# The last down stage: two PSUM tiles with two halves each, or eight banks with a quarter each

## The chip, the core and the metric

One core of a Trainium2 chip runs the whole kernel. The metric is the device time in microseconds (us) of one execution; the time of a kernel is the median over its runs.

## The reference

A retention layer feeds a mixture of four two-layer networks. Reduced to what matters here:

```python
# x: (4608, 512), the retention output of 8 batches x 576 tokens, heads side by side
p = domain_probs / (domain_probs.sum(-1, keepdims=True) + 1e-09)   # (4608, 4)
out = zeros((4608, 512))
for e in range(4):
    h = maximum(x @ w1[e], 0)          # w1[e]: (512, 1024)
    out += p[:, e:e+1] * (h @ w2[e])   # w2[e]: (1024, 512)
```

Inputs and output are float32. The kernel multiplies in bfloat16 and accumulates in float32.

## The kernel before

The 4608 tokens are nine tiles of 512 (`nt`), and for each tile there are four experts (`e`), so there are 36 stages. A stage has an up product (tokens times w1, then relu, into `hT`, hidden features on the partitions) and a down product (`hT` times w2). The down product of a stage is issued between the pieces of the up product of the next stage (`up_fast` and its `fill`), so that TensorE always has one to run while the other is being emptied. The order is written out by hand: every engine runs its instructions in the order in which the program issues them, and waits are semaphores between engines. The last stage (tile 8, expert 3) has no up product behind it, so its down product stands alone at the end of the program, in the loop at L1120 to L1136.

From the second tile on most products use a scheme with seven block products instead of eight. For the down product a set of 256 rows by 512 columns is cut into quarters 11, 12, 21 and 22 (rows: tokens in the first or the second half of the tile; columns: the first or the second 256 of 512). `Down` (L624) does this for one set of 128-token blocks; `s` is 0 or 1, and set `s` holds the token blocks `s` and `s + 2` of the tile. The parts of the scheme:

- Sums on VectorE beforehand: `hidden_sum` (L616, L618, L620, L622) makes sums of blocks of `hT`; `down_sums` has made sums of blocks of w2 (`dsum`).
- `product(i)`, i from 1 to 7: four matmuls of 128x128 by 128x256 each (L644). Products 1 and 2 add up quarter 11, 3 and 5 belong to quarter 12, and 4, 6 and 7 to quarters 21 and 22.
- `copy`: ScalarE copies product 1 into the place of the second row's sum ("P1", L650), so that product 6 adds onto it; it keeps product 5 in SBUF ("m5", L657) and the sum of products 1 and 6 ("U", L654).
- `add`: VectorE adds U to quarter 12 and m5 to quarter 22 (L661).
- `out`: a finished row of 512 columns is multiplied by the token's weight and added to `acc` (L673), since for the last tile (`on_chip`) the sum over the experts stays in SBUF; after the last expert it is sent to `out` (L680).

PSUM has eight banks, named P, Q, R, o0, o1, a0, a1 and a2. In `Down` the tile V holds quarters 11 and 12 in one bank, and W holds 21 and 22 in another. For the last stage set 0 has V in o0 and W in o1, which the stage before used for its own down product, and set 1 has them in P and Q, which the up product used. The banks a0, a1 and a2 were used by the attention and are idle by then. The loop at L1121 issues product 1 of both sets, then product 5 of both sets with the P1 and m5 copies behind each, then 6, 2, 7, 3 and 4. After product 3 the first row is finished in two halves, each with an accumulation on VectorE and a transfer of 128 KB issued by SP; after product 4 the second row likewise. All eight transfers go through SP's queue, which waits for VectorE ahead of each. The end of the program (L1162 in the profile) waits for all transfers on SP and joins the engines.

Of the kernel before, what the change touches and what calls it, by code (L numbers as in the profile page):

```python
# [9 lines left out]
FP32 = mybir.dt.float32  # L10
BF16 = mybir.dt.bfloat16
Copy = mybir.ActivationFunctionType.Copy
Relu = mybir.ActivationFunctionType.Relu
Exp = mybir.ActivationFunctionType.Exp
MULT = mybir.AluOpType.mult
ADD = mybir.AluOpType.add
# [7 lines left out]
def kernel(  # L24
# [10 lines left out]
    nc = tc.nc  # L35
    B, H, S, D = q.shape
    N, E = moe_domain_probs.shape
    _, Dm, F = moe_w1.shape
    assert (B, H, S, D) == (8, 8, 576, 64) and (N, E, Dm, F) == (4608, 4, 512, 1024)
    scale = 1.0 / math.sqrt(D)  # L40
    C = 128
    NCH = S // C
    R = S - NCH * C
# [3 lines left out]
    NFC = F // 128  # L47
    NT = 512
    n_nt = N // NT
    NSUB = NT // 128  # L50
# [7 lines left out]
    raw = ctx.enter_context(tc.tile_pool(name="raw", bufs=RAW))  # L58
# [5 lines left out]
    tpool = ctx.enter_context(tc.tile_pool(name="tpool", bufs=1))  # L64
# [12 lines left out]
    def one_bank(tag, shape, dtype, name):  # L77
        return psum.tile(shape, dtype, tag=tag, name=name)
# [63 lines left out]
    w1_sb, w2_sb = [], []  # L142
# [71 lines left out]
    probs = const.tile([128, E, NTT], FP32)  # L214
# [36 lines left out]
    class Att:  # L251


        def __init__(self, b):
            self.b, self.t = b, state[b]
            self.m, self.qkT, self.sT, self.s = {}, {}, {}, {}
# [243 lines left out]
    def on_chip(nt):  # L500
        return nt in (0, n_nt - 1)

    def out_pair(nt, e, pair, j):

        if e == 0 or not on_chip(nt):
            acc[nt, j] = apool.tile([128, 2, Dm], FP32, tag="acc", name="acc")
        return acc[nt, j]

    def send(nt, e, pair, j):
        x = slice(nt * NSUB + pair[0], nt * NSUB + pair[1] + 1, pair[1] - pair[0])  # L510
        if e == 0:
            i = nc.sync.dma_start(out=out_rows[:, x, :], in_=acc[nt, j])
        else:
            i = nc.gpsimd.dma_start(out=out_rows[:, x, :], in_=acc[nt, j], accum_op=ADD)  # L514
            for p, d in sent[nt, e - 1]:
                if set(p) & set(pair):
                    after(i, d)
        sent.setdefault((nt, e), []).append((pair, i))

    acc, hTs, tsum, ssum, dsum, hsum = {}, {}, {}, {}, {}, {}  # L520
# [57 lines left out]
    HF, HT, HD = F // 2, NT // 2, Dm // 2  # L578
# [28 lines left out]
    def hidden_sum(nt, e, i, g=None):  # L607

        lo, hi = (slice(2 * g, 2 * g + 2), slice(4 + 2 * g, 6 + 2 * g)) if g is not None else (slice(0, 4), slice(4, 8))
        hT = hTs[nt, e]  # L610
        a11, a12, a21, a22 = (hT[:, k, t] for t in (slice(0, HT), slice(HT, NT)) for k in (lo, hi))
        h = hsum.setdefault((nt, e), {})
        if i != 3 and i not in h:
            h[i] = hpool.tile([128, NFC // 2, HT], BF16, tag=f"hs{i}", name="hsum", bufs=1)
        if i == 1:
            nc.vector.tensor_tensor(h[1][:, lo], a21, a22, op=ADD)  # L616
        elif i == 2:
            nc.vector.tensor_tensor(h[2][:, lo], h[1][:, lo], a11, op=SUB)  # L618
        elif i == 3:
            nc.vector.tensor_tensor(a21, a11, a21, op=SUB)  # L620
        else:
            nc.vector.tensor_tensor(h[4][:, lo], a12, h[2][:, lo], op=SUB)  # L622

    class Down:  # L624

        def __init__(self, nt, e, s, tags=("o0", "o1")):
            self.nt, self.e, self.s, self.tags = nt, e, s, tags

        def product(self, i, part=slice(0, NFC // 2)):
            hT, h, w, t = hTs[self.nt, self.e], hsum[self.nt, self.e], w2_sb[self.e], dsum[self.e]
            lo, hi, a, b = slice(0, 4), slice(4, 8), slice(0, HD), slice(HD, Dm)
            if i == 1:
                self.V, self.W = (one_bank(x, [128, 2, HD], FP32, "down" + y) for x, y in zip(self.tags, "VW"))
            o, l, r = {1: (self.V[:, 0], hT[:, lo, :HT], w[:, lo, a]),
                       2: (self.V[:, 0], hT[:, hi, :HT], w[:, hi, a]),
                       3: (self.V[:, 1], h.get(4), w[:, hi, b]),
                       4: (self.W[:, 0], hT[:, hi, HT:], t[:, 2]),
                       5: (self.V[:, 1], h.get(1), t[:, 0]),  # L640
                       6: (self.W[:, 0], h.get(2), t[:, 1]),
                       7: (self.W[:, 0], hT[:, lo, HT:], w[:, lo, b])}[i]
            for k in range(NFC // 2)[part]:
                nc.tensor.matmul(o, lhsT=l[:, k, self.s * 128:(self.s + 1) * 128], rhs=r[:, k],  # L644
                                 start=(i == 1 and k == 0), stop=(k == NFC // 2 - 1), skip_group_check=True)

        def copy(self, what):

            if what == "P1":
                nc.scalar.activation(self.W[:, 0], self.V[:, 0], Copy)  # L650
            elif what == "U":
                self.u = tpool.tile([128, HD], FP32, tag="u" if self.tags[0] == "o0" else "ts", name="u",
                                    bufs=1 if self.tags[0] == "o0" else 2)
                nc.scalar.activation(self.u, self.W[:, 0], Copy)  # L654
            else:
                self.m5 = tpool.tile([128, HD], FP32, tag="m5d" if self.tags[0] == "o0" else "m5", name="m5d")
                nc.scalar.activation(self.m5, self.V[:, 1], Copy)  # L657

        def add(self, c):
            o, i, x = {12: (self.V[:, 1], self.V[:, 1], self.u), 22: (self.W[:, 1], self.W[:, 0], self.m5)}[c]  # L660
            nc.vector.tensor_tensor(o, i, x, op=ADD)  # L661

        def out(self, i, halves=(slice(0, 2),)):
            nt, e, j, pair = self.nt, self.e, self.s, (self.s, self.s + 2)
            if i == 0:
                out_pair(nt, e, pair, j)
            t, po, acc_ = nt * NSUB + pair[i], (self.V, self.W)[i], acc[nt, j][:, i]
            pe = probs[:, e, t:t + 1]
            for x in halves:
                cols = slice(x.start * HD, x.stop * HD)  # L670
                a, src = acc_[:, cols], po[:, x].rearrange("p a d -> p (a d)")
                if e and on_chip(nt):
                    nc.vector.scalar_tensor_tensor(a, src, pe, a, op0=MULT, op1=ADD)  # L673
                elif i == 1:
                    nc.scalar.activation(a, src, Copy, scale=pe)  # L675
                else:
                    nc.vector.tensor_scalar_mul(a, src, pe)  # L677
                if e == E - 1 and on_chip(nt):
                    eng = nc.scalar if len(halves) == 1 and x.start else nc.sync
                    eng.dma_start(out=out[t * 128:(t + 1) * 128, cols], in_=a)  # L680
            if i == 1 and not on_chip(nt):
                send(nt, e, pair, j)

    def up_fast(nt, e, g, fill, window, sums):
# [15 lines left out]
        P, Q, R_ = (one_bank(t, [128, 2, HT], FP32, "up" + t) for t in "PQR")  # L700
        m5 = tpool.tile([128, 2, HT], FP32, tag="m5", name="m5")
        product(P, lambda k: w[:, k, :HF], lambda k: x[:, k, t0], start=True)
        nc.scalar.activation(Q, P, Copy)  # L703
        product(R_, lambda k: s[:, 0, k], lambda k: T[:, 0, k], start=True)
        nc.scalar.activation(m5, R_, Copy)  # L705
        fill(1)
        sums(1)
        product(P, lambda k: s[:, 1, k], lambda k: T[:, 1, k])
        nc.vector.tensor_tensor(R_, P, m5, op=ADD)  # L709
        product(Q, lambda k: w[:, 2 + k, :HF], lambda k: x[:, 2 + k, t0])  # L710
# [18 lines left out]
    a0 = AttP(0)  # L729
# [271 lines left out]
    def stage(nt, e):  # L1001
        return nt * E + e
# [3 lines left out]
    for e in (3, 0):  # L1006

        use, last = stage(*begin[e]) + 1, stage(*begin[e]) - E + 2
# [10 lines left out]
    before, gaps = (1, 0), 0  # L1019
    for nt, e in [(nt, e) for nt in range(1, n_nt) for e in range(E)][1:]:  # L1020
# [96 lines left out]
        before = nt, e  # L1117
    for a in ((2, 1), (3,), (4,)):
        hidden_sum(*before, *a)
    ds = [Down(*before, s, tags) for s, tags in enumerate((("o0", "o1"), ("P", "Q")))]  # L1120
    for i in (1, 5, 6, 2, 7, 3, 4):  # L1121
        for d in ds:
            d.product(i)
            if i == 5:
                d.copy("P1")
                d.copy("m5")
            if i == 6:
                d.copy("U")
            if i == 2:
                d.add(12)  # L1130
            if i == 7:
                d.add(22)
            if i == 3:
                d.out(0, (slice(0, 1), slice(1, 2)))
            if i == 4:
                d.out(1, (slice(1, 2), slice(0, 1)))  # L1136


# [28 lines left out]
```

## Time and profile before

| | us |
|---|---|
| median of 4 runs | 517.59 |
| lowest and highest run | 516.79 and 518.62 |
| profiled execution, its own time | 522.04 |
| span of the profiled execution | 520.30 |
| TensorE busy in the span | 507.2 (97%) |
| VectorE, ScalarE, GpSimd busy | 377.0, 334.6, 247.1 |

The profile is of one execution: its span runs from the first to the last instruction, and 1.74 us of its own time lie around the span. Times in the profile are counted from the start of the span. PE is TensorE, DVE is VectorE, ACT is ScalarE, POOL is GpSimd, and SP is the engine that only issues transfers and waits. A chain of waits follows the work that ended last back to its cause. A row of the timeline gives the start, the duration, the engine, the line and the number of merged instructions. The last 14 us of the span are the part that the change touches.

### The profile page before, as it was taken

Reading aid. Unit: us, or ns where it says so; the run is one execution under the profiler, and the core shown is the slowest. Engines: PE = TensorE matmul, PEld = TensorE weight load, DVE = VectorE, ACT = ScalarE, POOL = GpSimd, SP = SyncE. Lnnn points to the kernel's source line nnn. Section 1 sums busy time; section 2 is a strip of 40 time slices with the busy share of each in tenths; the row PEclk is TensorE's granted clock in tenths of the full one; section 3 lists DMA queues with packets and bytes.
Section 4 is the critical chain, followed back from the end, with each engine's and each line's share of the span. In section 5 each row is a group of like instructions: output and inputs, shape, how many; then the busy total and the mean of one; then the engine's idle time right before and its main releaser. Section 6 shows DMA issues by size and latency. Waiting matters only on the chain.

```text
span 520.3 us, 12812 instructions
## 1 busy us (share of the span) xinstructions
PE 507.2 (97%) x4934; PEld 408.4 (78%) x4934; DVE 377.0 (72%) x700; ACT 334.6 (64%) x689; POOL 247.1 (47%) x341
## 2 busy tenths in 40 slices
PE   8999999999999999999999999999999999999995
PEld 3644455578788888888888888888888888888884
DVE  5722569969777777778777877786778777777775
ACT  3272352577677767667767777777677767776661
POOL 6702173747463666457644764476447521221100
PEclk9699999999999999999999999999999999999999
DMA  9999995959989599979999999889987652664002
GB/s 237 182 207 201 200 195 133 180 155 156 147 153 175 123 175 149 197 150 162 160 188 181 150 153 180 183 155 150 192 184 122 93 83 83 84 84 78 1 2 81
DMA packets 161037, 76.27 MB, mean 147 GB/s; under 512 B 131756, under 2 KB 145068, under 8 KB 160976
## 3 DMA queue, kind: packets, MB, share of 16 engines
q1 hardware_dynamic: 142224, 45.05, 45.8%
q0 software_dynamic: 18752, 30.41, 36.7%
q8 instruction: 38, 0.62, 0.5%
q14 instruction: 23, 0.19, 0.1%
HBM read 45.16 MB, written 31.46 MB: 147 GB/s over the span
## 4 chain that ended last, share of the span: by engine, by line
PE 93%; DVE 4%; DMA 2%; issue 1%; SPq 0%; ACT 0%; DVEq 0%
PE upP L697 20%; PE downV L644 20%; PE downW L644 15%; PE upR L697 10%; PE ph L525 7%; PE po L564 7%; PE upQ L697 5%; PE s L328 2%; PE oc L379 1%; PE oc L376 1%; PE kvp L346 1%; DMA qkT<-km 1%; DMA raw<-in_q_dram 1%; DVE acc L673 1%; PE warm_out L164 1%
## 5 line engine op out<-in xcount | busy, mean ns | idle before, releaser
L644 PEld LDWEIGHTS <-hT 128*128 128x128 bf16 x992 | 97.0, 98 | 11.8 <-issue 0.6
L697 PEld LDWEIGHTS <-wt 128*128 128x128 bf16 x992 | 94.9, 98 | 13.7 <-issue 1.7
L718 POOL TENSOR_SCALAR hT<-hT 128x512 bf16<-128x512 bf16 x62 | 38.0, 613 | 110.8 <-DVE hT L717 110.7
L644 PE MATMUL downV<-wt,hT 128*128 128x256 bf16 x496 | 83.9, 273 | 0.4 <-DVE acc L673 0.4
L697 PEld LDWEIGHTS <-wsum 128*128 128x128 bf16 x744 | 72.7, 98 | 10.8 <-issue 2.0
L644 PEld LDWEIGHTS <-hsum 128*128 128x128 bf16 x744 | 72.3, 98 | 9.4 <-DVE hsum L616 0.3
L709 DVE TENSOR_TENSOR upR<-upP,m 128x512 f32<-128x512 f32 x62 | 43.3, 698 | 46.4 <-ACT downW L650 41.2
L697 PE MATMUL upP<-xT,wt 128*128 128x256 bf16 x496 | 74.4, 273 | 1.3 <-DVE upR L709 1.3
L725 ACT ACTIVATE hT<-upP 128x512 bf16<-128x512 f32 x62 | 37.0, 597 | 51.8 <-PE upP L697 37.1
L514 POOL DMA_DIRECT2D out_dram<-acc x42 | 51.3, 1221 | 30.9 <-ACT acc L675 24.1
L677 DVE TENSOR_SCALAR acc<-downV,probs 128x512 f32<-128x512 f32 x56 | 41.9, 749 | 30.1 <-PE downV L644 29.7
L720 ACT ACTIVATE hT<-upR 128x512 bf16<-128x512 f32 x62 | 37.0, 597 | 31.0 <-PE upR L697 31.0
L717 DVE TENSOR_TENSOR hT<-upP,m 128x512 bf16<-128x512 f32 x62 | 42.8, 690 | 7.5 <-PE upP L697 6.4
L711 ACT ACTIVATE hT<-upQ 128x512 bf16<-128x512 f32 x62 | 37.0, 597 | 16.1 <-PE upQ L697 16.1
L675 ACT ACTIVATE acc<-downW,probs 128x512 f32<-128x512 f32 x56 | 38.6, 689 | 9.1 <-PE downW L644 9.1
L541 ACT ACTIVATE hT<-ph 128x512 bf16<-128x512 f32 x40 | 23.6, 597 | 31.7 <-PE ph L525 31.7
L340 POOL TENSOR_SCALAR_AFFINE_SELECT sT<-sT 128x512 bf16<-128x512 bf16 x24 | 15.1, 631 | 59.5 <-ACT sT L339 50.1
L697 PE MATMUL upR<-tsum,wsum 128*128 128x256 bf16 x248 | 37.2, 273 | 1.7 <-DVE tsum L592 1.7
L703 ACT ACTIVATE upQ<-upP 128x512 f32<-128x512 f32 x62 | 37.0, 597 | 2.5 <-PE upP L697 2.3
L525 PE MATMUL ph<-xT,wt 128*128 128x512 bf16 (+3 forms) x180 | 38.4, 372 | 0.0
L705 ACT ACTIVATE m<-upR 128x512 f32<-128x512 f32 x62 | 37.0, 596 | 1.2 <-PE upR L697 1.2
L697 PE MATMUL upP<-tsum,wt 128*128 128x256 bf16 x248 | 37.3, 273 | 0.0
(137 smaller groups left out, 1029.4 us busy)
## 6 DMA issues: line engine op xcount, KB each, us to landing
out_dram<-acc POOLq DMA_DIRECT2D x42, 512.0 KB, 6.6
out_dram<-acc SPq DMA_DIRECT2D x14, 512.0 KB, 3.6
wt<-in_moe_w_dram POOLq DMA_DIRECT2D x6, 1024.0 KB, 26.4
raw_k<-in_k_dram SPq DMA_DIRECT2D x24, 256.0 KB, 4.5
raw_q<-in_q_dram SPq DMA_DIRECT2D x24, 256.0 KB, 3.5
raw_v<-in_v_dram SPq DMA_DIRECT2D x24, 256.0 KB, 4.5
raw<-in_k_dram SPq DMA_DIRECT2D x8, 256.0 KB, 5.6
raw<-in_q_dram SPq DMA_DIRECT2D x8, 256.0 KB, 5.7
```

Of the source, the lines that this page charges most:

```text
L514: i = nc.gpsimd.dma_start(out=out_rows[:, x, :], in_=acc[nt, j], accum_op=ADD)
L525: nc.tensor.matmul(ph[:, ts], lhsT=w1_sb[e][:, dc, fc * 128:(fc + 1) * 128], rhs=xts[nt][:, dc, ts], start=(dc == 0), stop=(dc == NDC - 1))
L644: nc.tensor.matmul(o, lhsT=l[:, k, self.s * 128:(self.s + 1) * 128], rhs=r[:, k], start=(i == 1 and k == 0), stop=(k == NFC // 2 - 1), ski ...
L675: nc.scalar.activation(a, src, Copy, scale=pe)
L677: nc.vector.tensor_scalar_mul(a, src, pe)
L697: nc.tensor.matmul(ps[:, l], lhsT=wa(kc)[:, f:f + 128], rhs=xa(kc), start=(start and l == 0 and kc == 0), stop=(kc == 1), skip_group_check ...
L703: nc.scalar.activation(Q, P, Copy)
L705: nc.scalar.activation(m5, R_, Copy)
L709: nc.vector.tensor_tensor(R_, P, m5, op=ADD)
L711: nc.scalar.activation(hT[:, lo, t0], Q, Relu)
L717: nc.vector.tensor_tensor(h22, P, m5, op=ADD)
L718: nc.gpsimd.tensor_scalar(h22, h22, float("inf"), 0.0, op0=MIN, op1=MAX)
```

## The change

Each quarter of the last stage gets a PSUM bank of its own: set 0 has 11, 12, 21 and 22 in a0, a2, o1 and R; set 1 in a1, P, Q and o0. A class `Last` takes over the loop. ScalarE's copy of product 1 now follows product 1 at once, and the kept copy follows product 5. Quarter 11 is finished after product 2 and quarter 22 after product 7: ScalarE multiplies it by the token's weight into a scratch tile (`part`, in the buffers that the raw inputs used), and GpSimd adds that to `acc`. Quarters 12 and 21 are finished on VectorE as before. A row is sent as one transfer of 256 KB: the first rows of both sets through SP's queue, behind product 3, the second rows through ScalarE's queue, behind product 4. The order of the products stays.

```diff
-    ds = [Down(*before, s, tags) for s, tags in enumerate((("o0", "o1"), ("P", "Q")))]
+    class Last(Down):
+        def __init__(self, nt, e, s, tags):
+            self.nt, self.e, self.s = nt, e, s
+            self.c = {k: one_bank(t, [128, HD], FP32, "last") for k, t in zip((11, 12, 21, 22), tags)}
+
+        def product(self, i):
+            k, (l, r) = {1: 11, 2: 11, 3: 12, 5: 12}.get(i, 21), self.factors(i)
+            for n in range(NFC // 2):
+                nc.tensor.matmul(self.c[k], lhsT=l[:, n, self.s * 128:(self.s + 1) * 128], rhs=r[:, n],
+                                 start=(i in (1, 5) and n == 0), stop=(n == NFC // 2 - 1), skip_group_check=True)
+
+        def keep(self, k, tag, bufs):
+            t = tpool.tile([128, HD], FP32, tag=tag, name="kept", bufs=bufs)
+            nc.scalar.activation(t, self.c[k], Copy)
+            return t
+
+        def add(self, o, i, x):
+            nc.vector.tensor_tensor(self.c[o], self.c[i], x, op=ADD)
+
+        def out(self, k, eng=None):
+            i, x = (k - 11) // 10, (k - 11) % 10
+            t, row = self.nt * NSUB + 2 * i + self.s, acc[self.nt, self.s][:, i]
+            a = row[:, x * HD:(x + 1) * HD]
+            pe = probs[:, self.e, t:t + 1]
+            if k in (11, 22):
+                part = raw.tile([128, H * D], FP32, tag="raw", name="part")[:, :HD]
+                nc.scalar.activation(part, self.c[k], Copy, scale=pe)
+                nc.gpsimd.tensor_tensor(a, a, part, op=ADD)
+            else:
+                nc.vector.scalar_tensor_tensor(a, self.c[k], pe, a, op0=MULT, op1=ADD)
+            if eng:
+                eng.dma_start(out=out[t * 128:(t + 1) * 128, :], in_=row)
+
+    ds = [Last(*before, s, t) for s, t in enumerate((("a0", "a2", "o1", "R"), ("a1", "P", "Q", "o0")))]
     for i in (1, 5, 6, 2, 7, 3, 4):
-        for d in ds:
+        for s, d in enumerate(ds):
             d.product(i)
-            if i == 5:
-                d.copy("P1")
-                d.copy("m5")
-            if i == 6:
-                d.copy("U")
-            if i == 2:
-                d.add(12)
-            if i == 7:
-                d.add(22)
-            if i == 3:
-                d.out(0, (slice(0, 1), slice(1, 2)))
-            if i == 4:
-                d.out(1, (slice(1, 2), slice(0, 1)))
+            if i == 1:
+                nc.scalar.activation(d.c[21], d.c[11], Copy)
+            elif i == 5:
+                d.m5 = d.keep(12, ("m5d", "m5")[s], 1)
+            elif i == 6:
+                d.u = d.keep(21, ("u", "ts")[s], 1 + s)
+            elif i == 2:
+                d.add(12, 12, d.u)
+                d.out(11)
+            elif i == 7:
+                d.add(22, 21, d.m5)
+                d.out(22)
+            elif i == 3:
+                d.out(12, nc.sync)
+            else:
+                d.out(21, nc.scalar)
```

In `Down` itself the table of the factors moves into a function `factors`, and the arguments that only the last stage used (`tags` and `halves`) go away; for the other stages it issues the same instructions in the same order.

More of the change, by code (lines that the diff above doesn't have):

```diff
@@ L624, with __init__, factors, product @@
     class Down:
-        def __init__(self, nt, e, s, tags=("o0", "o1")):
-            self.nt, self.e, self.s, self.tags = nt, e, s, tags
-        def product(self, i, part=slice(0, NFC // 2)):
+        def __init__(self, nt, e, s):
+            self.nt, self.e, self.s = nt, e, s
+        def factors(self, i):
             hT, h, w, t = hTs[self.nt, self.e], hsum[self.nt, self.e], w2_sb[self.e], dsum[self.e]
             lo, hi, a, b = slice(0, 4), slice(4, 8), slice(0, HD), slice(HD, Dm)
+            return {1: (hT[:, lo, :HT], w[:, lo, a]), 2: (hT[:, hi, :HT], w[:, hi, a]), 3: (h.get(4), w[:, hi, b]),
+                    4: (hT[:, hi, HT:], t[:, 2]), 5: (h.get(1), t[:, 0]), 6: (h.get(2), t[:, 1]),
+                    7: (hT[:, lo, HT:], w[:, lo, b])}[i]
+        def product(self, i, part=slice(0, NFC // 2)):
             if i == 1:
[L635 to L642, printed above, removed]
+                self.V, self.W = (one_bank(x, [128, 2, HD], FP32, "down" + y) for x, y in zip(("o0", "o1"), "VW"))
+            o = self.V[:, i in (3, 5)] if i in (1, 2, 3, 5) else self.W[:, 0]
+            l, r = self.factors(i)
             for k in range(NFC // 2)[part]:
@@ L651, in copy @@
             elif what == "U":
-                self.u = tpool.tile([128, HD], FP32, tag="u" if self.tags[0] == "o0" else "ts", name="u",
-                                    bufs=1 if self.tags[0] == "o0" else 2)
+                self.u = tpool.tile([128, HD], FP32, tag="u", name="u")
                 nc.scalar.activation(self.u, self.W[:, 0], Copy)
             else:
-                self.m5 = tpool.tile([128, HD], FP32, tag="m5d" if self.tags[0] == "o0" else "m5", name="m5d")
+                self.m5 = tpool.tile([128, HD], FP32, tag="m5d", name="m5d")
                 nc.scalar.activation(self.m5, self.V[:, 1], Copy)
@@ L661, in add, with out @@
             nc.vector.tensor_tensor(o, i, x, op=ADD)
-        def out(self, i, halves=(slice(0, 2),)):
+        def out(self, i):
             nt, e, j, pair = self.nt, self.e, self.s, (self.s, self.s + 2)
@@ L666, in out @@
                 out_pair(nt, e, pair, j)
[L667 to L680, printed above, removed]
+            t, a = nt * NSUB + pair[i], acc[nt, j][:, i]
+            po, pe = (self.V, self.W)[i][:, :].rearrange("p a d -> p (a d)"), probs[:, e, t:t + 1]
+            if e and on_chip(nt):
+                nc.vector.scalar_tensor_tensor(a, po, pe, a, op0=MULT, op1=ADD)
+            elif i == 1:
+                nc.scalar.activation(a, po, Copy, scale=pe)
+            else:
+                nc.vector.tensor_scalar_mul(a, po, pe)
             if i == 1 and not on_chip(nt):
@@ L1119 @@
         hidden_sum(*before, *a)
-    ds = [Down(*before, s, tags) for s, tags in enumerate((("o0", "o1"), ("P", "Q")))]
+    class Last(Down):
+        def __init__(self, nt, e, s, tags):
+            self.nt, self.e, self.s = nt, e, s
+            self.c = {k: one_bank(t, [128, HD], FP32, "last") for k, t in zip((11, 12, 21, 22), tags)}
[23 more added lines that the diff above has]
+                eng.dma_start(out=out[t * 128:(t + 1) * 128, :], in_=row)
@@ L1121 @@
+    ds = [Last(*before, s, t) for s, t in enumerate((("a0", "a2", "o1", "R"), ("a1", "P", "Q", "o0")))]
     for i in (1, 5, 6, 2, 7, 3, 4):
-        for d in ds:
+        for s, d in enumerate(ds):
             d.product(i)
-            if i == 5:
-                d.copy("P1")
-                d.copy("m5")
-            if i == 6:
-                d.copy("U")
-            if i == 2:
-                d.add(12)
-            if i == 7:
-                d.add(22)
-            if i == 3:
-                d.out(0, (slice(0, 1), slice(1, 2)))
-            if i == 4:
-                d.out(1, (slice(1, 2), slice(0, 1)))
+            if i == 1:
[12 more added lines that the diff above has]
+                d.out(12, nc.sync)
+            else:
+                d.out(21, nc.scalar)
```

## The prediction

> **What bounds the kernel now.** I read the chain that ended last first, then the stretches of the last 14 us, then the timeline and DMA view there. The program order of the two kernels, engine by engine, differs only behind the last matmul of the stage before, so only the stretch from 506.5 us to the end can change. TensorE is busy in nearly all of the span, but not there:
>
> ```profile
> 506.60:507.70 1.10, 0.70 (x7) 0.49 (x5) 0.79 (x2) 0.47 (x1) 0.00 (x0) 1.00 0.00 0
> 507.70:509.60 1.90, 1.89 (x16) 1.56 (x16) 1.90 (x5) 0.38 (x2) 0.00 (x0) 1.00 0.00 0
> 509.60:514.30 4.70, 4.68 (x41) 3.79 (x39) 3.52 (x9) 1.50 (x5) 0.00 (x0) 1.00 0.00 0
> 514.30:516.30 2.00, 0.00 (x0) 0.00 (x0) 1.95 (x5) 0.00 (x0) 0.00 (x0) 1.00 0.66 228
> 516.30:518.60 2.30, 0.00 (x0) 0.00 (x0) 0.00 (x0) 0.00 (x0) 0.00 (x0) 0.97 0.77 261
> 518.60:520.30 1.70, 0.00 (x0) 0.00 (x0) 0.00 (x0) 0.00 (x0) 0.00 (x0) 0.50 0.00 0
> ```
>
> The columns are PE, PEld, DVE, ACT, POOL, clock, DMA share, GB/s. The reader is to see that POOL does nothing in the last 14 us, that after 514.3 VectorE alone computes, and that 4.3 us pass between the last matmul and the last byte. The chain of waits names the pieces:
>
> ```profile
> 506.91 0.76 DVE acc L673
> 507.67 0.04 issue
> 507.71 1.91 PE downV L644 x16
> 509.62 0.02 issue
> 509.64 1.17 PE downW L644 x8
> ...
> 514.68 0.39 DVEq L1162
> 515.08 1.18 DVE acc L673 x3
> ```
>
> TensorE stands until VectorE has emptied bank o0 (507.67), and stalls again ahead of product 6 (eight matmuls take 1.17 instead of 1.04). The timeline shows what follows the last product:
>
> ```profile
> 513.26 1.04 PE L644 MATMUL downW<-dsum,hT 128*128 128x256 bf16 x8
> 513.03 1.66 DVE L673 SCALAR_TENSOR_TENSOR acc<-downV,probs,acc 128x256 f32<-128x256 f32 x4
> 514.60 1.65 DVE L673 SCALAR_TENSOR_TENSOR acc<-downW,probs,acc 128x256 f32<-128x256 f32 x4
> 513.54 4.04 SPq L680 DMA_DIRECT2D out_dram<-acc  x8
> ```
>
> Eight quarter rows run one after another on VectorE, 0.39 us apart, to 516.25; eight transfers leave SP about 0.49 apart, the last at 517.16, so SP is 0.9 behind VectorE. In the DMA view bytes move from 514.4 to 518.6. The rows that price the new work:
>
> ```profile
> L279 POOL TENSOR_TENSOR km<-raw_k,gk 128x512 bf16<-128x512 f32 x24 | 25.8, 1076 | 0.5
> L675 ACT ACTIVATE acc<-downW,probs 128x512 f32<-128x512 f32 x56 | 38.6, 689 | 9.1 <-PE downW L644 9.1
> out_dram<-acc SPq DMA_DIRECT2D x4, 256.0 KB, 2.1
> out_dram<-acc SPq DMA_DIRECT2D x8, 128.0 KB, 1.8
> ```
>
> **The change, part by part.** Below, s0 and s1 are the two 128-token sets, P1 to P7 the products; times are on the clock of the profiled execution.
>
> *Own banks (a0, a1, a2 are idle since the attention ended).* P1 no longer waits for o0. Matmuls of this shape start 0.109 apart ((1.04 - 0.27)/7); the last of the stage before starts at 506.81 + 2 x 0.109 = 507.03, so P1 starts at 507.14 instead of 507.71: 0.57 sooner. P1 and P5 then take 16 x 0.109. P5's second half needs the second L616 sum (ready 507.99) at 508.23: no wait. That sum and the others on VectorE stay where they are, behind the two 0.75 us accumulations of the stage before.
>
> *P6.* It adds onto ScalarE's copy of P1. For s0 that copy goes into o1, which VectorE reads for the stage before until 508.65; so a wait on VectorE takes the place of the old wait on P5. Copy 508.74 to 509.11 (0.37, the L650 row), P6 at 509.16, while TensorE is ready at 508.89: 0.27 lost, where the old stage lost 0.31. Queued behind that copy on ScalarE are the s1 copy (done 509.42, needed 509.60), the two kept P5 copies and the two kept P6 copies (0.38 each, 0.28 apart; the last done 510.66, needed by P7 of s1 at 511.35). None is late.
>
> *The rest of TensorE.* P2, P7, P3, P4 follow without a gap: P3 of s0 at 511.78 needs the L622 sum (510.18) and the add into bank 12 (510.71); P4 needs the adds of bank 22 (done 511.98 and 512.42 after P7, needed at 512.66 and 513.09). The last matmul starts at 513.42 and ends at 513.69, against 514.30.
>
> *The quarters.* VectorE loses four of its eight quarter rows (4 x 0.39); quarters 11 and 22 go to ScalarE and POOL while TensorE still multiplies. VectorE keeps quarter 12 (512.42 and 512.82, behind P3 and the last add) and 21: 513.30 to 513.77 and, after the last matmul, 513.73 to 514.21. So VectorE ends at 514.21, not 516.25: 2.04 sooner.
> ScalarE's scaled copy is 0.43 to 0.47 (kept copy 0.38, plus half to all of the 0.09 by which the scaled 512-wide row exceeds the plain one): 510.68 and 511.11 for quarter 11, 512.02 and 512.45 for 22.
> POOL's add of 128x256: the trace has the two-operand POOL row at 512 wide only (1.076). Bounds 0.54 (half) and 1.08 (no scaling); one-operand POOL rows fall from about 0.63 at 512 wide to 0.42 at 256, a fixed part of 0.2, which makes it 0.62, and I take that. The four adds end at 513.7, 0.5 before VectorE's last quarter, so they cost nothing; cover gone, they would be on the path of the last transfer. At 1.08 they end at 515.5, the last transfer leaves 1.1 later and the last byte 0.4 later.
> Here a rule speaks against the change: the Trainium skill, GPSIMD Engine Reference, Engine selection, says an elementwise operation with two inputs belongs on VectorE because GpSimd takes about twice as long; its 2.6 cycles an element at 1.2 GHz are an estimate of 0.56 for 256. The row agrees (1.076 against VectorE's 0.70 at 512). By the rule the four quarters stay on VectorE: 4 x 0.39 there, some of it ahead of quarter 21, so the last byte is issued up to 1.5 later. But the slower engine is idle and ends first; the trace decides for the change.
>
> *The transfers.* Eight of 128 KB on SP become four of 256 KB, two on SP, two on ScalarE's own queue, which is empty by then. Issue when both halves of a row are done, plus 0.06 to 0.09 for the semaphore instruction: 512.99 and 513.43 on SP, 513.86 and 514.35 on ScalarE (0.38 to 0.5 each, as L680 and L559 take on SP). The last leaves 2.81 sooner (517.16 before).
> That is not the gain, for the transfers now press on each other. A transfer's first byte moves 0.85 after its issue (513.54 to 514.39), so bytes start at 513.84. Packets of 2 KB take 84 ns (the 512 KB sends of L512: 67% of 16 engines for 2 us, 256 packets); 512 of them on 16 engines are 2.69, and such a send needs 0.16 more than its packets (1.5 against 1.34): 2.85, so the last byte is at 516.69 if no engine starves. Before it was 518.60: 1.91 sooner.
> On the second queue the Trainium skill, DMA: Bandwidth & Descriptors, Issuing engines are not separate DMA queues, says that all queues end on the same 16 DMA engines and a second one saves only issue time. Here SP's lag of 0.9 is all that by this rule the queue can give; the rest comes from VectorE's 2.04 and from halving the number of issues. The sum above already shares the engines.
>
> *The end.* SP waits for its semaphores one after another, 0.06 apart. The transfer that ends last was third in that row, with seven behind it; now three are behind it: 0.24 less.
>
> Sum: 1.91 + 0.24 = 2.15. The span of 520.30 becomes 518.15. The profiled execution took 522.04 in all, 4.45 above the median of the runs (517.59); I take the difference over to the median: 515.4. A measurement of this kernel tells about 0.3% (1.55 us) from no change.
>
> **The rivals.**
> *Transfers keep their old pace (0.15).* Before, 1 MB took 4.2 from first to last byte, about 4.0 of it without the one gap. If two queues fill the engines no better than one (the DMA share was 0.66 to 0.77), the last byte is at 513.84 + 4.0 = 517.84: gain 0.76 + 0.24 = 1.0, time 516.6, within 0.3%. For it: the share never reached 0.9. Against: those gaps came from SP's issues, and the 512 KB sends run at 1.5.
> *POOL is late (0.06).* At 1.08 an add the gain is 2.15 - 0.43 = 1.7: 515.9. Against: half the elements.
> *ScalarE's queue starts badly (0.09), the slower one.* ScalarE issues no transfer before, so the first two on its queue are the last two of the kernel, with nothing to hide them. Lower bound: SP's very first issue took 1.13 to the first byte, 0.28 over 0.85; POOL's first took 1.8. A faster start than SP's is not excluded but would gain nothing past the engines' 2.85. Place: the third transfer, and the fourth behind it in order. With a delay X the last byte is at 514.35 + X + 0.85 + 0.82 = 516.02 + X; it passes 518.60 + 0.24 when X is over 2.8. At X = 4.9 the kernel takes 519.7. Nothing in the trace costs that much (SP's longest issue is 1.67), hence the small chance.
>
> **How the numbers follow.** The forecast has 0.70: 515.4, its own range 514.6 to 516.2 (gain 1.4 to 3.0: starved engines on one side, 0.2 less at P6 and fewer DMA gaps on the other). About a tenth of it falls within 0.3%. The range is 514.4 to 516.9, which takes in the first two rivals and leaves out the third and what lies below. Faster 0.63 + 0.04 (pace) + 0.04 (POOL) = 0.71; within 0.3% 0.07 + 0.11 + 0.02 = 0.20; slower 0.09.
>
> **What would show it.** In the profile after: first matmul of the last stage at about 507.1 with no wait on VectorE; a stall of 0.2 to 0.3 ahead of P6 released by ScalarE; last matmul about 0.6 sooner; VectorE's last quarter at 514.2; POOL adds of 0.6 ending before it; four transfers, the last issued at 514.35, the last byte near 516.7. It is wrong if the POOL row is over 1 us, if the ScalarE issues take over 1 us or their bytes start over 1.2 after issue, or if bytes flow for more than 3.3 us.

## The result, and the profile after

The change takes the median from 517.59 to 515.76 us. The ratio is 0.9969, with a 95% interval of 0.9961 to 0.9978, which is about 1.6 us of 517.6. (The two medians alone differ by 1.83.)

The profiled executions differ by more, 520.3 against 515.1 us of span. Most of that has nothing to do with the change. In both programs the same instructions run up to the last matmul of the stage before, and the execution before was behind by then: in one early stretch it was granted a slower clock (0.64 on the mean from 13 to 26 us, against 0.95 in the execution after). The clock row of the page before, then of the page after (40 slices, tenths of full speed):

```profile
PEclk9699999999999999999999999999999999999999
```

```profile
PEclk9999999999999999999999999999999999999999
```

So I read all traces by the **tail**: the time from the start of the last matmul of the stage before (the last one at L644) to the end of the span. Before it is 520.30 - 507.03 = 13.27 us, after it is 515.14 - 503.39 = 11.75: 1.52 less, which agrees with the ratio. "At 6.4" below means 6.4 us into the tail.

The timeline of the kernel after, one answer for each of PE, DVE, POOL, SP and ACT:

```profile
503.06 0.60 PE L644 MATMUL downW<-dsum,hT 128*128 128x256 bf16 x4
503.50 1.04 PE L1123 MATMUL last<-wt,hT 128*128 128x256 bf16 x8
504.37 2.18 PE L1123 MATMUL last<-dsum,hsum 128*128 128x256 bf16 x16
...
509.01 1.04 PE L1123 MATMUL last<-dsum,hT 128*128 128x256 bf16 x8
```

```profile
508.77 1.79 DVE L1144 SCALAR_TENSOR_TENSOR acc<-last,probs,acc 128x256 f32<-128x256 f32 x4
```

```profile
507.58 2.78 POOL L1142 TENSOR_TENSOR acc<-acc,part 128x256 f32<-128x256 f32 x4 [4.79 <-ACT part L1141]
```

```profile
509.33 0.82 SPq L1146 DMA_DIRECT2D out_dram<-acc  x2
```

```profile
505.10 0.65 ACT L1153 ACTIVATE last<-last 128x256 f32<-128x256 f32 x2 [1.68 <-DVE acc L669]
...
510.21 0.88 ACTq L1146 DMA_DIRECT2D out_dram<-acc  x2
```

The last stage starts at 0.11 with no wait (0.68 before). Sixteen matmuls of products 5 and 6 take 2.18 instead of 1.91, because ScalarE's copy waits for VectorE's accumulation of the stage before. VectorE's last quarter ends 0.52 after the last matmul's modelled end, not 1.95. And four transfers are issued within 1.8 us, where eight took 4.0. The DMA view of 510 to 514 us, 40 slices of 0.1 us:

```profile
DMA  0289999999999999999888999999941000100000
GB/s 0 102 328 348 369 369 451 389 369 328 348 389 451 369 369 328 328 389 533 348 348 348 389 369 389 389 369 369 389 164 41 20 20 20 41 0 0 0 0 0
...
q14 instruction: 1, 0.01, 0.5%
```

For 2.8 us nearly all of the 16 DMA engines are busy; before, with SP's issues 0.49 apart, the share in this stage was 0.66 to 0.77. Then, from 513.0 to 513.6, only 20 to 40 GB/s move: that is about one engine of sixteen (a full set moves about 370), still busy with its share. The packets say the same: each transfer closes with sixteen packets of 4 bytes, and of the last sixteen, fifteen end by 9.69 and one at 10.19. And among the packets there is one that is no output: an instruction packet on queue 14, from 8.46 to 8.77 into the tail.

| into the tail, us | before | predicted | after |
|---|---|---|---|
| first matmul of the last stage | 0.68 | 0.11 | 0.11 |
| gap ahead of product 6 | 0.31 in all | 0.27 | 0.27 |
| last matmul starts | 6.99 | 6.39 | 6.39 |
| POOL's last add ends | none | 6.67 | 6.97 |
| VectorE's last quarter ends | 9.22 | 7.18 | 7.18 |
| last transfer issued | 10.13 | 7.32 | 7.32 |
| last byte | 11.57 | 9.66 | 10.18 |
| SP past the wait for it | 11.94 | 10.03 | 10.68 |
| end | 13.27 | 11.12 | 11.75 |

(The columns before and after are the starts and ends in the trace less 507.03 and 503.39; the predicted ones are the prediction's times less 507.03, and 10.03 is its last byte and the 0.37 of before.) Every step down to the last issue came out within 0.01 us, but for POOL, which is off the path. The bytes and their end did not: 0.63 of the 2.15 is missing there.

### The profile page after: what moved, and what is told of

Read it like the earlier page. It is cut to its first block, busy times and chain, and to the rows that moved or that the text cites. A ratio compares the mean times of both kernels' runs of the same rounds, so it can differ in the third digit from the quotient of the medians.

```text
span 515.1 us, 12811 instructions
## 1 busy us (share of the span) xinstructions
PE 502.0 (97%) x4934; PEld 406.3 (79%) x4934; DVE 374.9 (73%) x696; ACT 336.3 (65%) x693; POOL 250.1 (49%) x345
## 4 chain that ended last, share of the span: by engine, by line
PE 87%; DMA 5%; DVE 3%; POOL 1%; issue 1%; SPq 1%; ACT 0%; DVEq 0%; ACTq 0%; POOLq 0%
PE upP L690 19%; PE downV L644 19%; PE downW L644 14%; PE upR L690 10%; PE po L564 7%; PE ph L525 6%; PE upQ L690 5%; DMA qkT<-km 4%; PE s L328 2%; PE oc L376 1%; PE oc L379 1%; PE kvp L346 1%; DMA raw<-in_q_dram 1%; DVE sT L469 0%; PE last L1123 0%
## 5 line engine op out<-in xcount | busy, mean ns | idle before, releaser
L644 PEld LDWEIGHTS <-hT 128*128 128x128 bf16 x960 | 93.9, 98 | 10.9
L644 PE MATMUL downV<-wt,hT 128*128 128x256 bf16 x480 | 81.8, 273 | 0.0
L644 PEld LDWEIGHTS <-hsum 128*128 128x128 bf16 x720 | 70.0, 98 | 8.7 <-DVE hsum L616 0.3
L690 PE MATMUL upP<-tsum,wsum 128*128 128x256 bf16 x248 | 37.2, 273 | 0.0
```

The costliest lines, as they stand in the source:

```text
L690: nc.tensor.matmul(ps[:, l], lhsT=wa(kc)[:, f:f + 128], rhs=xa(kc), start=(start and l == 0 and kc == 0), stop=(kc == 1), skip_group_check ...
```

## The experiments

Each kernel is the change with one edit, unless it says otherwise. Its tail is from its own trace; the ratio is to the kernel before.

| kernel | tail, us | ratio (95% interval) |
|---|---|---|
| before | 13.27 | 1 |
| the change | 11.75 | 0.9969 (0.9961 to 0.9978) |
| e1, banks only | 12.61 | 0.9983 (0.9962 to 1.0004) |
| e2, all quarters on VectorE | 12.82 | 0.9998 (0.9978 to 1.0017) |
| e3, eight transfers on SP | 12.26 | 0.9996 (0.9974 to 1.0018) |
| e4, four transfers on SP | 11.75 | 0.9961 (0.9945 to 0.9976) |
| e5, code fetch moved | 11.12 | 0.9956 (0.9940 to 0.9972) |
| e6, banks exchanged | 11.47 | 0.9972 (0.9961 to 0.9983) |
| e7, POOL doubled | 12.40 | 0.9992 (0.9982 to 1.0001) |
| e8, combined | 10.41 | 0.9942 (0.9927 to 0.9958) |

The times of single kernels scatter by several tenths of a per cent, so the tails decide here, and the ratios only for e8. Each tail is of one execution, but steps that kernels share repeat closely: the last matmul starts at 6.39 in the change, e1, e3, e4, e5 and e7.

**e1: own banks only**

The quarters go to VectorE as in e2 below, and in the order of before:

```diff
-                eng.dma_start(out=out[t * 128:(t + 1) * 128, :], in_=row)
+                eng.dma_start(out=out[t * 128:(t + 1) * 128, x * HD:(x + 1) * HD], in_=a)
...
                 d.add(12, 12, d.u)
-                d.out(11)
...
                 d.add(22, 21, d.m5)
-                d.out(22)
...
+                d.out(11, nc.sync)
                 d.out(12, nc.sync)
             else:
-                d.out(21, nc.scalar)
+                d.out(22, nc.sync)
+                d.out(21, nc.sync)
```

> Own banks and the early copies kept; all eight quarters finished by VectorE behind products 3 and 4, and eight transfers of 128 KB by SP, as before. Measure: the tail, from the start of the last matmul of the stage before to the end of the span (13.27 us before the change, 11.75 after). Theory (the end of the kernel is a line of last matmul, quarters, issues, bytes): the banks move TensorE's last matmul 0.6 earlier, VectorE's queue and SP's eight issues 0.49 apart follow it, so the tail is 12.6 to 12.8. Rival (the banks alone bring most of the gain, the rest is cosmetic): 11.9 to 12.1.

```profile
513.17 3.22 DVE L1139 SCALAR_TENSOR_TENSOR acc<-last,probs,acc 128x256 f32<-128x256 f32 x8
```

```profile
513.68 4.10 SPq L1141 DMA_DIRECT2D out_dram<-acc  x8
```

Tail 12.61: 0.66 less than before, the 0.6 that TensorE gained. VectorE's eight quarters and SP's eight issues are as long as before; they only start sooner. The theory holds.

**e2: all quarters on VectorE, early and in four transfers**

```diff
-            if k in (11, 22):
-                part = raw.tile([128, H * D], FP32, tag="raw", name="part")[:, :HD]
-                nc.scalar.activation(part, self.c[k], Copy, scale=pe)
-                nc.gpsimd.tensor_tensor(a, a, part, op=ADD)
-            else:
-                nc.vector.scalar_tensor_tensor(a, self.c[k], pe, a, op0=MULT, op1=ADD)
+            nc.vector.scalar_tensor_tensor(a, self.c[k], pe, a, op0=MULT, op1=ADD)
```

> The change with quarters 11 and 22 finished by VectorE too (no ScalarE copy with the weight, no POOL add); the four transfers on two queues stay. Theory: VectorE's eight quarters run 0.39 apart and end 0.85 later, the first row is ready 0.9 later, and the bytes follow: tail 12.5 to 12.7. Rival (the quarters on POOL at 0.72 end so late that they gain little): 11.8 to 12.0.

```profile
508.18 2.05 DVE L1139 SCALAR_TENSOR_TENSOR acc<-last,probs,acc 128x256 f32<-128x256 f32 x5
```

Tail 12.82, 1.07 more than the change, a little above what was expected. VectorE ends at 8.13 instead of 7.18, and the first transfer leaves at 6.98 instead of 5.95; the bytes then need the same 3.4 us. So POOL pays, although an add takes 0.72 there against 0.47 for a quarter on VectorE. A row of 512 columns can only leave when both its quarters are done, so what POOL takes off VectorE lets the first row leave 1.03 sooner, and the tail is 1.07 shorter for it.

**e3: eight transfers of 128 KB, all on SP**

```diff
-                eng.dma_start(out=out[t * 128:(t + 1) * 128, :], in_=row)
+                for y in range(2):
+                    eng.dma_start(out=out[t * 128:(t + 1) * 128, y * HD:(y + 1) * HD], in_=row[:, y * HD:(y + 1) * HD])
...
-                d.out(21, nc.scalar)
+                d.out(21, nc.sync)
```

> The change with eight transfers of 128 KB, all on SP, in place of four of 256 KB on two queues. Theory: the first can leave 1 us sooner (quarter 11 is ready early), but SP issues the other seven 0.49 apart from 5.9 on, the last at 8.9 after the start of the tail, and the last byte is 1.4 behind it: tail 12.0 to 12.2. Rival (only the bytes count): they start 1 us sooner and end sooner, tail 11.0 to 11.3.

```profile
508.33 4.59 SPq L1147 DMA_DIRECT2D out_dram<-acc  x8
```

Tail 12.26, 0.51 more than the change and 0.06 above what was expected. The first transfer leaves 1.0 sooner, the last at 9.14, after seven more issues that SP makes 0.43 to 0.95 apart; its last byte is 1.43 behind that. Had only the bytes counted, this kernel would have been faster. Read with e1 and e2, the parts depend on each other: with eight transfers the early quarters on ScalarE and POOL bring 0.34 (12.61 to 12.26), with four they bring 1.07 (12.82 to 11.75). (The comparison is not quite even: e1 finishes quarter 11 behind product 3, e2 behind product 2.)

**e4: four transfers, all on SP**

```diff
-                d.out(21, nc.scalar)
+                d.out(21, nc.sync)
```

> The change with all four transfers of 256 KB on SP. Theory: SP takes 0.36 for an issue and the rows come 0.43 to 0.5 apart, so nothing queues; the engines carry the same bytes: tail 11.5 to 11.9, no change. Rival (a second queue shares the engines better): tail 12.2 or more.

```profile
509.66 2.08 SPq L1146 DMA_DIRECT2D out_dram<-acc  x4
```

Tail 11.75, the same to the hundredth, though the third transfer leaves 0.39 and the fourth 0.33 later than on ScalarE's queue. So the tail came out as expected, but not the step to it: SP did hold two rows back. The engines are full at that time, so ScalarE's queue brings nothing here and costs nothing. It also shows what decides with four transfers: when the first row leaves, as long as the later ones leave before the engines run dry (in e7 below they do run dry). One engine is 0.5 late here too, so that does not come from sharing the engines between two queues.

**e5: SP's code fetch moved**

```diff
+    for _ in range(24):
+        nc.sync.drain(fusable=False)
+
     class Last(Down):
```

> The change with 24 drain instructions put into SP's stream behind the last transfer of the tile before, some 75 us ahead of the tail, where SP idles. They do no work; they shift where in SP's stream its next block of code is fetched. In the change's trace one 8 KB instruction packet moves at 8.46 after the start of the tail, in the middle of the output's bytes, and one of the 16 DMA engines ends 0.5 behind the others (98.5% of the packets done at 9.68, the last at 10.18). Theory (SP's code fetch holds that engine up): no such packet in the window, last byte at 9.65 to 9.75, tail 11.2 to 11.3. Rival (the late engine comes from how two queues or four transfers are shared out): last byte 10.1 to 10.2, tail 11.7.

The DMA view of 509.5 to 513.5 us of this kernel, slices of 0.1 us as above:

```profile
DMA  0037999999999999999998999998983000000000
GB/s 0 0 143 307 410 369 430 410 348 328 369 389 451 389 369 369 369 328 471 369 369 348 410 349 451 369 369 348 410 328 123 0 0 0 0 0 0 0 0 0
```

No instruction packet is left in that window, the rate falls from full to nothing without the long end, and the last byte is at 9.66 instead of 10.18. SP is past its wait 0.38 later, as before the change, where in the change it took 0.49. The tail is 11.12: 0.63 less, better than expected by that shorter wait, and equal to the forecast's 13.27 - 2.15. The packet has not gone, it came sooner. At 69.8 us ahead of the tail, some 0.4 us after the last of the 24 drains, this kernel fetches two instruction packets where the change fetches one (queue 14 in 433 to 433.8 us of e5, then in 433.4 to 434.2 us of the change):

```profile
q14 instruction: 2, 0.02, 4.8%
```

```profile
q14 instruction: 1, 0.01, 2.4%
```

So the fetched block was SP's own: instructions added to SP's stream alone moved it. What sets the moment of a fetch is not shown.

**e6: banks o1 and R exchanged**

```diff
-    ds = [Last(*before, s, t) for s, t in enumerate((("a0", "a2", "o1", "R"), ("a1", "P", "Q", "o0")))]
+    ds = [Last(*before, s, t) for s, t in enumerate((("a0", "a2", "R", "o1"), ("a1", "P", "Q", "o0")))]
```

> The change with banks o1 and R of set 0 exchanged: quarter 21 in R, which is free, quarter 22 in o1. Theory: ScalarE's first copy no longer waits for VectorE's last accumulation of the stage before (5.0 after the start of the tail), product 6 follows product 5 without the gap of 0.27, and everything behind it, the bytes too, is 0.27 earlier: last matmul 6.11, tail 11.4 to 11.5. Rival (another wait, ScalarE's own queue or the VectorE sums, takes its place): last matmul 6.3 to 6.4, tail 11.65 to 11.75.

```profile
502.74 1.91 PE L1123 MATMUL last<-dsum,hsum 128*128 128x256 bf16 x16
```

```profile
502.57 0.74 ACT L1153 ACTIVATE last<-last 128x256 f32<-128x256 f32 x2 [0.77 <-PE last L1123]
```

ScalarE's copy now waits for the matmul alone, the sixteen matmuls take 1.91, and everything behind is 0.27 earlier: last matmul at 6.11, tail 11.47. The gap ahead of product 6 was that bank and nothing else.

**e7: a second add on POOL ahead of each**

```diff
-                part = raw.tile([128, H * D], FP32, tag="raw", name="part")[:, :HD]
+                both = raw.tile([128, H * D], FP32, tag="raw", name="part")
+                part, more = both[:, :HD], both[:, HD:]
                 nc.scalar.activation(part, self.c[k], Copy, scale=pe)
+                nc.gpsimd.tensor_tensor(more, part, part, op=ADD)
                 nc.gpsimd.tensor_tensor(a, a, part, op=ADD)
```

> The change with a second add of the same size on POOL ahead of each of its four (its result goes to unused scratch and nothing reads it). Theory: POOL's chain of four adds of 0.69 ends only 0.2 ahead of VectorE, so doubled it ends at 9.7 after the start of the tail and sets the last row: last issue 9.8, tail 12.9 to 13.1, nearly all of the gain gone. Rival (POOL is well hidden): tail 11.7 to 12.0.

```profile
L1144 POOL TENSOR_TENSOR acc<-acc,part 128x256 f32<-128x256 f32 x4 | 2.9, 723 | 0.0
L1143 POOL TENSOR_TENSOR part<-part 128x256 f32<-128x256 f32 x4 | 2.4, 612 | 4.8 <-ACT part L1142 4.8
```

Tail 12.40: 0.65 more than the change, where 1.2 to 1.4 was expected. The direction is the theory's, the size is only half: the added one is cheaper (0.61; it reads one operand twice, which may be why), so POOL ends at 9.25, not 9.7, and of the 1.95 by which the last transfer leaves later only 0.76 reaches the last byte. By then the other three are through, and the last has all the engines to itself: issued at 9.28, last byte at 10.94, 1.67 later, where in the change it took 2.86. The DMA view of 508 to 513 us of this kernel, slices of 0.125 us, has the pauses:

```profile
DMA  0029999924989883000398989200078999600000
```

**e8: the parts put together**

e5's drains, e6's banks, and:

```diff
                 nc.gpsimd.tensor_tensor(a, a, part, op=ADD)
+                if k == 11:
+                    nc.sync.dma_start(out=out[t * 128:(t + 1) * 128, :HD], in_=a)
...
-                eng.dma_start(out=out[t * 128:(t + 1) * 128, :], in_=row)
+                cols = slice(HD if k == 12 else 0, Dm)
+                eng.dma_start(out=out[t * 128:(t + 1) * 128, cols], in_=row[:, cols])
```

> A version meant to beat both: the change with the banks exchanged as in the run before last, SP's code fetch moved, and quarter 11 sent alone (128 KB on SP) as soon as POOL has it, quarter 12 alone too; the second rows stay two transfers of 256 KB on ScalarE's queue. Theory: bytes start at 5.5 after the start of the tail instead of 6.8, the last row leaves at 7.05, the last byte is at 8.8 to 9.0, tail 10.4 to 10.7: about 1.1 less than the change, 0.2% of the time. Rival (six transfers cost in issues and end waits what the early start brings): tail 11.0 or more, no better than the two first parts together.

Its DMA view of 508 to 512.2 us, slices of 0.105 us:

```profile
DMA  0006997102999558993699999999999899951000
...
q1 hardware_dynamic: 576, 0.52, 36.1%
q10 hardware_dynamic: 288, 0.52, 32.7%
```

The first rows start to move at 5.5 instead of 6.8, quarter by quarter and with gaps, and the second rows then fill the engines to the end. The last byte is at 9.09, the tail 10.41, 1.34 less than the change. The gains of e5 and e6 together would leave 10.85 (11.75 - 0.63 - 0.27, an estimate), so the early sends are worth about 0.44. The median is 514.53 us, and the interval of its ratio, 0.9927 to 0.9958, lies below that of the change (0.9961 to 0.9978). This version beats both.

## Why the prediction was right, and where it was short

*What bounds the stage, and the order of the steps.* Right. The tail is a line of last matmul, quarters, issues and bytes; the wait for bank o0, the new wait ahead of product 6 (0.27), the 2.04 that VectorE gains and the times of all four issues came out as worked out. e1, e2 and e6 each move a link, and what is behind it moves by as much, within about 0.1. What the forecast left open is that VectorE's 2.04 does not reach the end by itself: its sum counts the bytes from the first transfer on, and e4 shows that the last one could leave 0.33 later at no cost.

*POOL.* The add was sized at 0.62 from one-operand rows; it is 0.72, with 0.69 from one to the next. That puts POOL's end at 6.97 instead of 6.67 and leaves 0.2 of the 0.5 of cover. The error cost nothing because the cover took it, which was luck in part: it used up 0.3 of the 0.5, and e7 shows what lies beyond. The forecast weighed the Trainium skill's rule (GPSIMD Engine Reference, Engine selection) that an elementwise operation with two inputs belongs on VectorE. The rows here have POOL slower by 1.5 to 1.7 times (0.72 us against 0.47 for a quarter and 0.43 for a plain add of this size on VectorE, 1.08 against 0.70 at 512 columns) and not twice, so the forecast's word that its row agrees is too strong; and the page's rate, with its estimate of 0.56 for this add, fell short of 0.72, as did the forecast's own 0.62. For this stage the rule does not hold: following it costs 1.07 (e2), for the slower engine was idle.

*The second queue.* The forecast gave it at most SP's lag, by the rule of the Trainium skill (DMA: Bandwidth & Descriptors, Issuing engines are not separate DMA queues) that all queues run on the same engines and a second one saves only issue time; this case agrees, for e4 has the same tail without it. The slower rival, a bad start of ScalarE's queue, did not happen: its issues took 0.38 each, and the fourth transfer's last byte came no later than on SP.

*The bytes.* This is the term that was mis-sized. The forecast had 2.85 us for 1 MB "if no engine starves". The bulk took about that, 2.90 from 6.79 to 9.69; but one engine was held up, and the last byte came after 3.39, which is beyond the 3.3 that the prediction named as the point where it would be wrong. The forecast's low side had engines starved of work; this one had work of another kind that the forecast left out. 0.52 of the shortfall is that engine and 0.11 the wait behind it; e5 takes both away by moving SP's code fetch alone. The packet itself took 309 ns; from 7.84 to 9.14, around it, five output packets took 118 to 191 ns, where the usual one takes 84 and none in e5 over 104. How these add up to 0.5 on one engine is not shown, for the records do not name the engine.

Before the change there was such a packet too (481 ns, at 8.39, also in the middle of the output), and it seems to have hurt little: the last sixteen closing packets ended at 11.42 to 11.58, with no engine apart. The view of 513.5 to 519 us before, slices of 0.1375 us, shows why that is likely, for the engines had gaps between the transfers in which a late one can catch up:

```profile
DMA  0000003994798303995798499569948974993000
...
q14 instruction: 1, 0.01, 0.5%
```

In e7, where a pause ahead of the last transfer gives such slack back, the fetch at 8.44 leaves no late engine either (closing packets at 10.80 to 10.95). No run takes the fetch out of the kernel before.

*The end.* SP's waits behind the last byte: 1.07 from passing the wait to the end, as forecast (1.09).

*The first rival, transfers at their old pace,* is not what happened: the engines did fill (nearly every slice reads 9). The gain came out between its 1.0 and the forecast's 2.15 from another cause. *The second rival, POOL late,* has the figures nearest to the measured ones (a gain of 1.7, 515.9 us), but not for its reason: the adds took 0.72 and not 1.08 us, and were off the path.

*The size.* The forecast's 2.15 was 0.63 too much by the tail; 1.5 to 1.6 is at the low edge of its own range of 1.4 to 3.0. A gain of 0.31% also lies on the line of 0.3% below which it called a gain hard to tell from none; the interval, 0.22 to 0.39%, excludes no change.

## What to carry to other kernels

At the end of a kernel nothing hides a wait, so list its links (last product, evacuation, issues, bytes, final waits) with a clock time for each, and look for the one behind which the others queue; where the bytes fill the DMA engines, that is the first send and not the last. An idle slow engine is worth using when it ends before the fast one would. When an edit removes the gaps from a transfer phase, the next limit is the slowest of the DMA engines and not their mean: look for anything else they carry. Read small changes by the stretch that the change can reach, measured from a common instruction, and not by two spans.

## What the runs showed of the hardware that was not expected

- SP's code came over the same 16 DMA engines as the data. With one 8 KB instruction packet (309 ns) in a full transfer of 1 MB, one of them ended 0.5 us behind, in the change, e2, e4 and e6 alike; with the fetch moved, no engine was late.
- POOL's add of two 128x256 float32 operands takes 0.72 us, where a 128x512 multiply into bfloat16 (L279) takes 1.08: half the elements, two thirds of the time.
- Instructions that do no work can change a kernel's end: 24 drains in SP's stream, some 70 us ahead of the tail and off its path, made it 0.63 us shorter, for they moved a code fetch.
